# A four-fold row fold for the Fourier step of sketched attention, with mirrored output rows and a new order of issue

## The chip, the cores and the metric

The kernel runs on one NeuronCore of one Trainium2 chip. The metric is the device time of one execution in microseconds (us). The engines are TensorE (PE, with its weight loads PEld), VectorE (DVE), ScalarE (ACT), GpSimd (POOL) and SyncE (SP, which issues most DMAs).

## What is computed

Linear attention with sketched features, for batch 4, 4 heads, 1088 rows and head width 32, then a Fourier mix and a small MLP on rows of 128 (cut from the reference):

```
phi(x) = outer(S1 x, S2 x)                     # 8 x 8 = 64 features
kv = sum_s phi(k) v ;  z = sum_s phi(k)
attn = (phi(q) kv) / (phi(q) z + 1e-6)         # heads side by side: x is (4, 1088, 128)
mixed = real(fft(fft(x, axis=1), axis=2))
u = x + mixed
un = (u - mean(u)) / sqrt(var(u) + 1e-6)
out = u + relu(un @ w_ch1) @ w_ch2             # 128 -> 512 -> 128
```

## The kernel before

All work is a list of named steps (`add(name, engine, reads, writes, emit)`). `ORDER` is a list of all step names written out by hand: the instructions of each engine, and the DMAs of SP's queue, are issued in that order. `ENGINE` moves a step to another engine than its default, `BANK` gives each PSUM use its bank, `BEHIND` makes a load wait for an earlier DMA of SP's queue, `AFTER` adds single waits, and `FILL` puts matmuls on zeros (`zeros`, L88 and L90) in front of a step.

**Attention.** For each batch b, `ld_k`, `ld_v` and `ld_q` (L123, L127, L141) load the inputs, DVE transposes k and q in blocks of 32 (`kT`, L379; `qT`, L428), PE makes the features (`kproj`, L361; `qfeat`, L435), ACT copies them out of PSUM (`kab`, `qa`), and POOL or DVE forms the products (`kp`, L102; `qp`, L446). PE sums kv and z (`kv`, L395), and numerator and denominator (`pnd`, L481). DVE takes the reciprocal (`rden`, L493) and writes x in bf16 (`xx`, L496). Each half of the 1088 rows gives four tiles, rows 4p to 4p + 3 on partition p; the 32 rows left of each half (`ld_qt`, `qt_T`, `qt_f`, `qt_a`, `qt_p`) form a ninth tile.

**Row transform.** `dfold` (df) adds and subtracts mirrored columns of x (nine tiles, 567 columns an instruction), and `fold` (eo) adds and subtracts the halves, rows r and r + 544 (516 columns), which leaves four tiles for even and four for odd frequencies. `srow` (s) multiplies them with tables of cosines and sines: for each of the four tiles, and once for the ninth, six matmuls of 272 to 274 columns (L521), 30 for a batch. The tables come from `t_turn`, `t_ph`, `t_pm`, `t_sin`, `t_cos` and `t_neg`, those of the ninth tile from `l_...`. `zev` (z) copies the spectrum out of PSUM; `zrev` (zr) writes it once more backwards with signs for the second half of the rows; `zlast` (zl) picks the columns of the ninth tile.

**Mixer.** Groups g = 0 to 9 follow: for each batch and half a group of four tiles (g = 0, 1, 2, 3, 5, 6, 7, 8), and for each pair of batches a group of one tile (g = 4 and 9). In each, `mix` adds x and the column transform in PSUM (L574, L577), `bn`, `var`, `sd`, `rc` and `un` normalize, `xt` transposes by DMA on SP's queue (L635; g up to 6, later groups use PE: `tr` and `ut`), `ph` and `rl` are the hidden layer and its relu (L643, L650, L652), `po` adds the output layer into the same PSUM bank (L657), and `fin` copies it to an `ot` buffer, of which the large groups share four. `own` (L559) names the buffers in turn. Then SP stores: `st_main` (L668) one DMA of 256 KB, 128 partitions of 2 KB, for a large group; `st_half` (L664) two DMAs, one from SP and one from ACT, for g = 8; `st_last` (L672) four DMAs of 16 KB for a group of one tile. Their patterns in DRAM, outermost dimension first:

```
L668  [[4 * DM, 128], [1, 4 * DM]]
L665  [[4 * DM, 128], [1, 2 * DM]]
L672  [[HALF * DM, 2], [2 * DM, 16], [1, DM]]      # x 4
```

The stores stand in `ORDER`, and so on SP's queue, among the transposes: xt0, xt1, xt2, out0, xt3, xt4, xt5, xt6, out2, out3, out1, out4, out5, out6, out9, out7, out8.0, with out8.1 on ACT.

Of the kernel before, what the change touches and what calls it, by code (L numbers as in the profile page):

```python
# [17 lines left out]
DM = H * D  # L18
# [4 lines left out]
LAST = HALF - 512  # L23
QD = DM // 2
NK = HALF // 2 + 1
NB = NK // 2 + 1
BY_DMA = (0, 1, 2, 3, 4, 5, 6)
SPLIT = {}
TURNS = {"un": 5, "unT": 5, "ht": 3, "ot": 4, "st": 5, "sm": 5}
NXD = 1  # L30
# [14 lines left out]
def view(t, offset, dims, p0=0, n=128):  # L45

    a = t[:]
    step = a.ap[0][0]
    return bass.AP(tensor=a.tensor, offset=a.offset + p0 * step + offset,
                   ap=[[step, n]] + [list(d) for d in dims])  # L50
# [6 lines left out]
def program(nc, T, x, bank):  # L57
# [82 lines left out]
    def ld_q(b, half):  # L140
        return [nc.sync.dma_start(view(T(f"q_in{b % 3}"), 4 * H * D * half, [[4 * D, H], [1, 4 * D]], p, n),  # L141
                                  dram(x["q"], (b * H * S + half * HALF + 4 * p) * D, [[4 * D, n], [S * D, H], [1, 4 * D]]))
                for p, n in parts(f"ld_q{b}.{half}", 128)]

    def ld_qt():

        return [nc.sync.dma_start(view(T("qt_in"), 0, [[D, B * H], [1, D]], 32 * par + 16 * half, 16),  # L147
                                  dram(x["q"], (512 + HALF * half + par) * D, [[2 * D, 16], [S * D, B * H], [1, D]]))
                for par in range(2) for half in range(2)]
# [31 lines left out]
    def c_iota():  # L181
        first = nc.gpsimd.iota(T("pi")[:], pattern=[[0, 1]], base=0, channel_multiplier=1)

        nc.gpsimd.iota(T("sr")[:], pattern=[[1, 6]], base=0, channel_multiplier=4,
                       allow_small_or_imprecise_dtypes=True)
        return first
    add("c_iota", POOL, "", "iota", c_iota)

    def c_kk():
# [7 lines left out]
    add("c_rows", DVE, "iota", "rows", lambda: nc.vector.tensor_scalar(  # L197
        out=T("sq")[:, 0:4], in0=T("sr")[:, 0:4], scalar1=1.0 / S, scalar2=None, op0=ALU.mult))

    def c_more():  # L200
        v = nc.vector
        pi, pa, sr = T("pi"), T("pa"), T("sr")
        for i, bits in enumerate((15, 16, 32, QD - 1)):
            v.tensor_scalar(out=pa[:, i:i + 1], in0=pi[:], scalar1=bits, scalar2=None, op0=ALU.bitwise_and)

        v.tensor_scalar(out=sr[:, 5:6], in0=pa[:, 0:1], scalar1=2.0, scalar2=512.0, op0=ALU.mult, op1=ALU.add)
        v.scalar_tensor_tensor(out=sr[:, 5:6], in0=pa[:, 1:2], scalar=HALF / 16.0, in1=sr[:, 5:6], op0=ALU.mult, op1=ALU.add)
        v.scalar_tensor_tensor(out=sr[:, 4:5], in0=pa[:, 2:3], scalar=1 / 32.0, in1=sr[:, 5:6], op0=ALU.mult, op1=ALU.add)
        v.tensor_copy(sr[:, 5:6], pa[:, 3:4])
# [23 lines left out]


    base = lambda: view(T("kk"), 0, [[NK, 2], [1, NB]])
    for i, t in enumerate((0, 2, 1, 3)):
        add(f"t_turn{t}", POOL, "rows kk", f"pha/{t}", lambda i=i, t=t: turn(T("ph")[:, i, :], t, base(), S))
        add(f"t_ph{t}", DVE, f"pha/{t} rows", f"phb/{t}", lambda i=i, t=t: rest(T("ph")[:, i, :], t, base()))
    W = 2 * NB
    add("t_pm0", DVE, "phb/0 phb/2", "pm", lambda: size(T("pm")[:], T("ph")[:, 0:2, :]))  # L240
    add("t_sin0", ACTE, "phb/0 phb/2 tabsin", "tab/S0", lambda: sin(view(T("tab"), W, [[4 * W, 2], [1, W]]), T("ph")[:, 0:2, :], S))
    add("t_cos0", ACTE, "pm hpi tabsin", "tab/C0", lambda: cos(view(T("tab"), 0, [[4 * W, 2], [1, W]]), T("pm")[:], S))
    add("t_sin1", ACTE, "phb/1 phb/3 tabsin", "tab/S1", lambda: sin(
        view(T("tab"), 3 * W, [[4 * W, 2], [1, W]]), view(T("ph"), 3 * W, [[-W, 2], [1, W]]), S))
    add("t_cos1", ACTE, "phb/1 phb/2 phb/3 tabsin", "tab/C1", lambda: sin(
        view(T("tab"), 2 * W, [[4 * W, 2], [NB, 2], [1, NB]]), view(T("ph"), 2 * W + NB - 2, [[W, 2], [NB + 1, 2], [-1, NB]]), S))


    add("a_sin", ACTE, "hpi", "tabsin", lambda: nc.scalar.activation(out=T("scr")[:, 0:1], in_=T("hpi")[:, 0:1], func=ACT.Sin))
    add("a_sqrt", ACTE, "hpi wd0 tab/S0 tab/S1 tab/C0 tab/C1 tabL/S tabL/C", "tabsqrt", lambda: nc.scalar.activation(  # L250
        out=T("scr")[:, 1:2], in_=T("hpi")[:, 0:1], func=ACT.Sqrt))

    def t_neg(engine):
        return (nc.vector if engine == DVE else nc.gpsimd).tensor_scalar(
            out=T("tab")[:, 8:12, :], in0=T("tab")[:, 4:8, :], scalar1=-1.0, scalar2=None, op0=ALU.mult)
    add("t_neg", eng("t_neg", DVE), "tab/S0 tab/S1 tab/C0 tab/C1", "neg", lambda: t_neg(eng("t_neg", DVE)))


# [12 lines left out]
    def d_trig():  # L271
        for c in range(2):
            lo, hi = slice(QD * c, QD * c + QD), slice(QD - QD * c, 2 * QD - QD * c)
            nc.scalar.activation(out=T("wd")[lo, c, :], in_=T("dpm")[lo, :], func=ACT.Sin, scale=-2 * PI / DM, bias=T("hpi")[lo, 0:1])
            nc.scalar.activation(out=T("wd")[hi, c, :], in_=T("dph")[hi, :], func=ACT.Sin, scale=-2 * PI / DM)
    add("d_trig", ACTE, "dphb dpm hpi tabsin", "wd0", d_trig)

    def d_alt(engine):

        done = []  # L280
        for c in range(2):
            p = QD - QD * c
            for i in range(2):
                done.append(memset(engine, view(T("wd"), DM * c + i, [[2, QD]], p, 1), 1.0 - 2 * i))
# [3 lines left out]
    add("d_alt", eng("d_alt", POOL), "wd0 sgn0", "wd", lambda: d_alt(eng("d_alt", POOL)))  # L288
    add("c_sgn", eng("c_sgn", POOL), "", "sgn0", lambda: memset(eng("c_sgn", POOL), T("sgn")[:], 1.0))
    def c_xd(i, e):  # L290
        memset(e, view(T(f"xd{i}"), 9 * (2 * QD + 1), [[1, QD - 1]]), 0.0)
        return memset(e, view(T(f"xd{i}"), QD, [[2 * QD + 1, 9]]), 0.0)
# [3 lines left out]
    for i in range(3):  # L296
        e = eng(f"c_eo{i}", POOL)
        add(f"c_eo{i}", e, "" if i < 2 else "tab/S0 tab/S1 tab/C0 tab/C1", f"eo0/{i}", lambda i=i, e=e: memset(e, view(T(f"eo{i}"), 2 * QD + 1, [[3 * QD, 8], [1, QD - 1]]), 0.0))
# [7 lines left out]
    add("c_id16", ACTE, "idb", "id16", lambda: nc.scalar.copy(T("id16")[:], T("idb")[0:16, 0:16]))  # L306

    def c_cen(engine):
        if engine == ACTE:
            nc.scalar.activation(out=T("cen")[:], in_=T("idb")[:], func=ACT.Identity, bias=T("less")[:, 0:1])  # L310
        else:
            nc.vector.tensor_scalar(out=T("cen")[:], in0=T("idb")[:], scalar1=-1.0 / DM, scalar2=None, op0=ALU.add)
    add("c_cen", eng("c_cen", ACTE), "idb hpi", "cen", lambda: c_cen(eng("c_cen", ACTE)))

    def c_mask():
# [6 lines left out]
    add("c_idb", POOL, "", "idb", lambda: eye(T("idb")[:], 128))  # L322

    add("c_qtp", eng("c_qtp", POOL), "", "qtp0", lambda: memset(
        eng("c_qtp", POOL), view(T("qtp"), 64, [[256, 4], [1, 128]]), 0.0))
# [8 lines left out]
    for i in range(2):  # L334
# [4 lines left out]
    add("s_t", PE, "s12/0 s12/1 id16 warm", "pST", lambda: nc.tensor.transpose(  # L339
        ps("st", 0, [[1, 16]]), T("s12")[:], T("id16")[:]), "st")  # L340
# [89 lines left out]
    def qfeat(b, pr):  # L430

        for w, src in enumerate(("sa", "sb")):
            for g in range(4):
                for h in range(2):
                    nc.tensor.matmul(  # L435
                        ps(f"q{b}.{pr}", 512 * g + 256 * w, [[1, 256]], 64 * h, 64),
                        view(T(src), 0, [[1, F]], 32 * g, 32),
                        view(T(f"qT{b % 2}"), 128 * (2 * pr + h), [[512, 2], [1, 128]], 32 * g, 32),
# [26 lines left out]
    def qt_p():  # L465

        for j in range(2):
            nc.vector.tensor_tensor(
                out=view(T("qtp"), 32 * j, [[256, 4], [192, 2], [1, 32]]), in0=ps("qt", 512 * j + 256, [[64, 4], [32, 2], [1, 32]]),
                in1=view(T("qta"), 256 * j, [[64, 4], [32, 2], [1, 32]]), op=ALU.mult)  # L470
    add("qt_p", DVE, "pqt qta qtp0", "qtp", qt_p, "qt:2")

    def pnd(b):
        for s in range(9):
            for pr in range(2):
                for c in range(2):
                    if s < 8:
                        w = view(T(f"qp{b % 2}"), 1024 * pr + 128 * s + 64 * c, [[1, 64]])
# [21 lines left out]

    def dfold(b, engine, w):

        X, Y = T(f"x{b}"), T(f"xd{b % NXD}")
        n = 2 * QD + 1
        if w == 0:
            copy(engine, view(Y, 0, [[n, 9], [2 * QD, 2]]), view(X, 0, [[DM, 9], [QD, 2]]))
        return tt(engine, view(Y, QD * w + 1, [[n, 9], [1, QD - 1]]), view(X, 1, [[DM, 9], [1, QD - 1]]),
                  view(X, DM - 1, [[DM, 9], [-1, QD - 1]]), (ALU.add, ALU.subtract)[w])

    def fold(b, engine, w):  # L510
        X, n = T(f"xd{b % NXD}"), 2 * QD + 1
        return tt(engine, view(T(f"eo{b % 3}"), 12 * QD * w, [[3 * QD, 4], [1, n]]), view(X, 0, [[n, 4], [1, n]]), view(X, 4 * n, [[n, 4], [1, n]]), (ALU.add, ALU.subtract)[w])

    def srow(b):


        def six(weights, movs, start, stop):
            for c, part in ((0, 0), (0, 1), (1, 1), (1, 0), (1, 2), (0, 2)):
                p, mov = QD * (c ^ (part > 0)), movs[c][part == 1]
                n = mov.ap[-1][1] * (mov.ap[-2][1] if len(mov.ap) > 2 else 1)  # L520
                nc.tensor.matmul(ps(f"z{b}", 512 * c + c, [[1, n]], p, QD), weights[c][:, QD * part:QD * part + QD], mov,  # L521
                                 start=start and part < 2, stop=stop, tile_position=(0, p), skip_group_check=True)

        six([view(T(f"xd{b % NXD}"), 8 * (2 * QD + 1), [[1, 3 * QD]])] * 2,
            [[view(T("tabl"), 2 * NK * trig + (NK - 1 if c == 0 else 0), [[1, NK + 1 - c]]) for trig in range(2)] for c in range(2)],
            True, False)

# [374 lines left out]
```

## Time and profile before

| what | us |
|---|---|
| median of three runs (82.05 to 82.67) | 82.61 |
| the profiled execution | 82.32 |
| its span, first to last instruction | 80.4 |
| PE busy | 69.6 |
| DVE busy | 65.0 |
| ACT busy | 49.5 |
| POOL busy | 45.2 |
| first output (out0) issued | 55.84 |
| last output (out8.1) issued | 77.57 |

A row of the timeline gives start, length, engine, line, operation and tiles. A digit of a DMA line is the busy share of the 16 DMA engines in one of 40 equal slices, in tenths (9 is 90% or more), and the GB/s line under it what they moved.

### The profile page before, as it was taken

Reading aid. Unit: us, or ns where it says so; the run is one execution under the profiler, and the core shown is the slowest. Engines: PE = TensorE matmul, PEld = TensorE weight load, DVE = VectorE, ACT = ScalarE, POOL = GpSimd, SP = SyncE. Lnnn points to the kernel's source line nnn. Section 1 sums busy time; section 2 is a strip of 40 time slices with the busy share of each in tenths; the row PEclk is TensorE's granted clock in tenths of the full one; section 3 lists DMA queues with packets and bytes.
Section 4 is the critical chain, followed back from the end, with each engine's and each line's share of the span. In section 5 each row is a group of like instructions: output and inputs, shape, how many; then the busy total and the mean of one; then the engine's idle time right before and its main releaser. Section 6 shows DMA issues by size and latency. Waiting matters only on the chain.

```text
span 80.4 us, 3294 instructions
## 1 busy us (share of the span) xinstructions
PE 69.6 (87%) x1368; PEld 52.0 (65%) x1375; DVE 65.0 (81%) x178; ACT 49.5 (62%) x85; POOL 45.2 (56%) x84
## 2 busy tenths in 40 slices
PE   4998693799999999999999999989997969797930
PEld 2323552489799766878788789956674837583720
DVE  5895879999869999999759699999878659894800
ACT  6244576475693645479692285609978548979530
POOL 6888579975857499597999619149850010000000
PEclk9999999999999999999999999999999999999999
DMA  0969998379929659556015003030500466133042
GB/s 8 270 174 269 229 288 208 53 208 229 227 44 310 207 144 292 151 125 212 0 34 43 0 8 65 8 65 0 177 19 16 95 190 253 29 130 138 24 176 90
DMA packets 16095, 10.47 MB, mean 130 GB/s; under 512 B 6864, under 2 KB 14544, under 8 KB 16080
## 3 DMA queue, kind: packets, MB, share of 16 engines
q1 hardware_dynamic: 15896, 10.13, 47.0%
q8 instruction: 10, 0.16, 0.8%
q10 hardware_dynamic: 184, 0.14, 0.5%
q14 instruction: 5, 0.04, 0.2%
HBM read 7.22 MB, written 2.23 MB: 117 GB/s over the span
## 4 chain that ended last, share of the span: by engine, by line
PE 48%; DVE 18%; DMA 11%; SPq 8%; ACT 7%; issue 4%; DVEq 0%; ACTq 0%
PE ps L481 9%; PE ps L395 8%; PE ps L435 7%; PE ps L657 6%; DMA t_qt_in<-in_q_dram 6%; PE ps L643 5%; DMA t_unT__166<-t_un__161 5%; PE ps L361 4%; SPq L141 3%; ACT t_ht__168 L650 3%; PE ps L521 2%; PE ps L458 2%; SPq L147 2%; DVE t_x__130 L496 2%; DVE t_x__131 L496 2%
## 5 line engine op out<-in xcount | busy, mean ns | idle before, releaser
L102 POOL TENSOR_TENSOR t_kp__119<-t_ab__117 128x512 f32<-128x512 f32 x7 | 7.3, 1068 | 1.5 <-ACT t_ab__117 L413 1.1
L650 ACT ACTIVATE t_ht__167<-ps 128x1024 bf16<-128x1024 f32 x6 | 6.0, 1022 | 1.6 <-PE ps L481 1.6
L102 POOL TENSOR_TENSOR t_kp__118<-t_ab__116 128x512 f32<-128x512 f32 x6 | 6.3, 1069 | 1.0 <-ACT t_ab__116 L413 1.0
L442 ACT COPY t_qa__122<-ps 128x1024 f32<-128x1024 f32 x4 | 4.1, 1013 | 3.1 <-DVE t_qp__124 L446 1.9
L650 ACT ACTIVATE t_ht__168<-ps 128x1024 bf16<-128x1024 f32 x4 | 4.1, 1024 | 2.9 <-PE ps L577 1.9
L442 ACT COPY t_qa__123<-ps 128x1024 f32<-128x1024 f32 x4 | 4.1, 1014 | 2.3 <-PE ps L435 2.3
L643 PEld LDWEIGHTS <-t_w1b 128*128 128x128 bf16 x40 | 3.0, 97 | 3.7 <-issue 1.5
L90 PE MATMUL ps<-t_wz 128*128 128x512 bf16 x12 | 5.0, 526 | 0.0
L481 PEld LDWEIGHTS ps<-t_kvz,t_qp__124 128*64 128x64 f32 x128 | 4.0, 137 | 0.9 <-ACT t_kvz L95 0.4
L481 PE MATMUL ps<-t_kvz,t_qp__124 128*64 128x66 f32 x128 | 4.4, 223 | 0.1
L395 PE MATMUL ps<-t_v__121,t_kp__119 128*64 128x33 f32 x128 | 4.3, 223 | 0.1
L102 POOL TENSOR_TENSOR t_eo__133<-t_xd__132 128x516 bf16<-128x516 bf16 x4 | 4.2, 1052 | 0.4 <-DVE t_xd__132 L102 0.3
L395 PEld LDWEIGHTS ps<-t_v__121,t_kp__119 128*64 128x64 f32 x128 | 4.1, 138 | 0.4 <-POOL t_zl__143 L96 0.4
L395 PE MATMUL ps<-t_v__120,t_kp__118 128*64 128x33 f32 x128 | 4.3, 223 | 0.0
L481 PEld LDWEIGHTS ps<-t_kvz,t_qp__125 128*64 128x64 f32 x128 | 3.9, 137 | 0.5 <-issue 0.4
L481 PE MATMUL ps<-t_kvz,t_qp__125 128*64 128x66 f32 x128 | 4.2, 223 | 0.0
L395 PEld LDWEIGHTS ps<-t_v__120,t_kp__118 128*64 128x64 f32 x128 | 4.1, 138 | 0.1
L650 ACT ACTIVATE t_ht__169<-ps 128x1024 bf16<-128x1024 f32 x4 | 4.0, 1027 | 0.0
L652 DVE TENSOR_SCALAR t_ht__168<-ps 128x1024 bf16<-128x1024 f32 x2 | 2.5, 1225 | 1.7 <-PE ps L657 1.0
L435 PE MATMUL ps<-t_qT__115,t_sa 32*64 32x256 f32 x64 | 2.8, 400 | 1.2 <-DVE t_qp__124 L446 1.2
L379 DVE STREAM_TRANSPOSE t_kT__112<-t_k_in__105 128x512 f32<-128x512 f32 (+1 forms) x3 | 2.7, 886 | 1.1 <-DMA t_k_in__105<-in_k_dram 1.1
L361 PE MATMUL ps<-t_sblk,t_kT__112 128*64 128x64 f32 x64 | 2.5, 226 | 1.1 <-DVE t_kT__112 L379 1.1
(266 smaller groups left out, 216.6 us busy)
## 6 DMA issues: line engine op xcount, KB each, us to landing
t_q_in__109<-in_q_dram SPq DMA_DIRECT2D x4, 256.0 KB, 3.3
t_v_in__107<-in_v_dram SPq DMA_DIRECT2D x8, 128.0 KB, 3.6
t_k_in__106<-in_k_dram SPq DMA_DIRECT2D x2, 512.0 KB
t_v_in__108<-in_v_dram SPq DMA_DIRECT2D x8, 128.0 KB, 3.3
t_k_in__105<-in_k_dram SPq DMA_DIRECT2D x2, 256.0 KB
t_q_in__110<-in_q_dram SPq DMA_DIRECT2D x2, 256.0 KB, 6.6
t_q_in__111<-in_q_dram SPq DMA_DIRECT2D x2, 256.0 KB
t_k_in__105<-in_k_dram SPq DMA_DIRECT2D x1, 512.0 KB
```

Source lines behind the costliest of these rows:

```text
L90: nc.tensor.matmul(T("ps")[:, free, :], w[:, 0:128], bass.AP(tensor=w.tensor, offset=w.offset, ap=[list(w.ap[0]), [0, 4], [1, 128]]), star ...
L102: return (nc.vector if engine == DVE else nc.gpsimd).tensor_tensor(out=out, in0=in0, in1=in1, op=op)
L361: nc.tensor.matmul(ps(use, 64 * t, [[1, 64]], 64 * c, 64), view(src, 128 * t + 64 * c, [[1, 64]]), T("sblk")[:], start=True, stop=True, ti ...
L379: nc.vector.transpose(view(T(f"kT{b % 2}"), 128 * lo, [[1, 128 * n]]), view(T(f"k_in{b % 2}"), D * lo, [[D, n], [8 * D, 4], [1, D]]))
L395: nc.tensor.matmul(ps(f"kv{b}", 33 * pr, [[1, 33]], 64 * c, 64), kp, v, start=(t == 0), stop=(t == 8), tile_position=(0, 64 * c), skip_gro ...
L435: nc.tensor.matmul(ps(f"q{b}.{pr}", 512 * g + 256 * w, [[1, 256]], 64 * h, 64), view(T(src), 0, [[1, F]], 32 * g, 32), view(T(f"qT{b % 2}" ...
L442: nc.scalar.copy(T(f"qa{pr}")[:], ps(f"q{b}.{pr}", 0, [[512, 4], [1, 256]]))
L481: nc.tensor.matmul(ps(f"nd{b}", 512 * (s // 3) + 132 * (s % 3) + 66 * pr, [[1, 66]], 64 * c, 64), w, view(T("kvz"), 132 * b + 66 * pr, [[1 ...
L496: nc.vector.tensor_tensor(out=view(T(f"x{b}"), 0, [[384, 3], [32, 12], [1, 32]]), in0=ps(f"nd{b}", 0, [[512, 3], [33, 12], [1, 32]]), in1= ...
L643: nc.tensor.matmul(ps(use, 128 * n * i, [[1, 128 * n]]), T("w1b")[:, 128 * c:128 * c + 128], own("unT", g)[:, 0:128 * n], start=True, stop ...
L650: nc.scalar.activation(out=out, in_=in_, func=ACT.Relu)
L657: nc.tensor.matmul(ps(u, ut_at(g, t), [[1, 128]]), view(own("ht", g), (128 if g % 5 == 4 else 512) * c + 128 * t, [[1, 128]]), T("w2b")[:, ...
```

## The change

Rows r, 544 - r, 544 + r and 1088 - r now lie on one partition, or on mirrored columns of it. Partitions 0 to 63 hold rows 1 + 4p on of a half, partitions 64 to 127 the rows from 288 of that half, whose order `qfeat` reverses with steps of -1. Rows 0 and 544, and 257 to 272 with their mirrors, are the ninth tile. A new fold, `mfold` (mf), adds and subtracts neighbouring tiles of x, mirrored rows; `dfold` and `fold` then run on fewer columns, and `srow` needs two sets of six matmuls and the ninth tile's six: 18 for a batch. The tables shrink, `t_far` mirrors them. `zev` writes the spectrum in two steps, in the order in which `mix` reads it; `zrev` is one copy, read backwards, and the signs are in a second set of column weights (`d_neg`). `zlast` reads PSUM. Each `ld_q` is two DMAs of 64 partitions, `ld_qt` is five, each `st` is two DMAs of 128 KB, and `st_last` is three. `ENGINE`, `FILL`, `BEHIND`, `AFTER`, `ORDER` and `BANK` are new throughout; `BY_DMA` is as before. The core of the diff:

```diff
     def ld_q(b, half):
-        return [nc.sync.dma_start(view(T(f"q_in{b % 3}"), 4 * H * D * half, [[4 * D, H], [1, 4 * D]], p, n),
-                                  dram(x["q"], (b * H * S + half * HALF + 4 * p) * D, [[4 * D, n], [S * D, H], [1, 4 * D]]))
-                for p, n in parts(f"ld_q{b}.{half}", 128)]
+        return [nc.sync.dma_start(view(T(f"q_in{b % 3}"), 4 * H * D * half, [[4 * D, H], [1, 4 * D]], 64 * far, 64),
+                                  dram(x["q"], (b * H * S + half * HALF + (FAR if far else 1)) * D,
+                                       [[4 * D, 64], [S * D, H], [1, 4 * D]])) for far in range(2)]
...
+    def mfold(b, engine, w):
+        X = T(f"x{b}")
+        return tt(engine, view(T(f"xm{b % NXM}"), 5 * DM * w, [[DM, 5], [1, DM]]), view(X, 0, [[2 * DM, 5], [1, DM]]),
+                  view(X, DM, [[2 * DM, 5], [1, DM]]), (ALU.add, ALU.subtract)[w])
...
-        use = (((0, 0), (1, 1)), ((2, 11), (7, 2)), ((4, 8), (5, 9)), ((10, 3), (3, 6)))
-        for t in range(4):
-            six([view(T(f"eo{b % 3}"), 3 * QD * (4 * c + t), [[1, 3 * QD]]) for c in range(2)],
...
+        table = ((2, 0), (1, 3))
+        for a in range(2):
+            six(lambda c, part: view(T(f"eo{b % 3}"), 6 * QD * c + 3 * QD * a + QD * part, [[1, QD]]),
+                [[view(T("tab"), W * table[a][trig] + TW * (1 - c), [[1, NK - c]]) for trig in range(2)] for c in range(2)],
+                False, a == 1)
...
+    def zev(b, half, engine):
+        copy(engine, view(T(f"z{b}"), 256 * half, [[128, 2], [64, 2], [1, 64]]),
+             ps(f"z{b}", *((512, [[-511, 2], [1, 2], [2, 64]]) if half == 0 else (783, [[-512, 2], [-1, 2], [-2, 64]]))))
     def zrev(b, engine):
+        return copy(engine, view(T(f"z{b}"), 512, [[128, 4], [1, 128]]), view(T(f"z{b}"), 127, [[128, 4], [-1, 128]]))
...
-    def st_main(b, half, g):
-        return [nc.sync.dma_start(dram(x["out"], (b * S + half * HALF) * DM, [[4 * DM, 128], [1, 4 * DM]]),
-                                  own("ot", g)[:])]
+    def st(b, half, g, w):
+        row = ((1, HALF + 1), (HALF + FAR, FAR))[half][w]
+        return (nc.sync, nc.scalar)[g == TWO and w == 1].dma_start(
+            dram(x["out"], (b * S + row) * DM, [[2 * DM, 2], [4 * DM, 64], [1, 2 * DM]]), own("ot", g)[:, 256 * w:256 * w + 256])
     def st_last(i, g):
-        return [nc.sync.dma_start(dram(x["out"], ((2 * i + j // 2) * S + 512 + j % 2) * DM, [[HALF * DM, 2], [2 * DM, 16], [1, DM]]),
-                                  own("ot", g)[32 * j:32 * j + 32, 0:128]) for j in range(4)]
+        def rows(first, n, p0):
+            return nc.sync.dma_start(dram(x["out"], (2 * i * S + first) * DM, [[2 * DM, n], [HALF * DM, 4], [1, DM]]),
+                                     own("ot", g)[p0:p0 + 4 * n, 0:128])
+        return [rows(257, 16, 64), rows(258, 15, 4), rows(0, 1, 0)]
...
 FILL = {
-    "warm": (1, 1, 6), "qf0.1": (0, 2, 6), "qf0.0": (0, 3, 6), "kpr1": (0, 1, 7), "po8.0": (0, 1, 0),
+    "s_t": (1, 0, 0), "qf0.1": (1, 1, 0), "qf1.0": (0, 2, 6), "kt_pr": (0, 1, 6), "pnd0": (0, 2, 5), "pnd1": (0, 2,
+    4), "po8.0": (0, 1, 2),
 }
```

The new order of the first loads on SP is k0.1, S1, q0.0, q0.1, q1.0, q1.1, k0.0, k1, v0.1, qt, kt. On PE the first output layer, po0, stands behind s1 and ahead of mix4, mix2, pnd3, ph1, mix3, s2 and ph4.0; po1, mix5, po4 and ph2.0 follow that. The stores and transposes on SP now come as xt0, xt1, out0, xt4, xt2, xt3, out4, xt5, out1, xt6, out2, out5, out3, out6, out9, out7, out8.0, with out8.1 on ACT.

## The prediction

> **What bounds the kernel now.** I read the page first, then the table of stages, the chain in order of time, the SP queue in the timeline, and the DMA view of two short windows. The profiled execution took 82.32 us, 0.29 under the median of 82.61; its span is 80.4, so 1.92 lies around it. I sum against 82.32.
>
> ```profile
> span 80.4 us, 3294 instructions
> ...
> PE 69.6 (87%) x1368; PEld 52.0 (65%) x1375; DVE 65.0 (81%) x178; ACT 49.5 (62%) x85; POOL 45.2 (56%) x84
> ...
> PE 48%; DVE 18%; DMA 11%; SPq 8%; ACT 7%; issue 4%; DVEq 0%; ACTq 0%
> ```
>
> ```profile
> 20.00:30.00 10.00, 9.94 (x293) 8.25 (x289) 8.78 (x12) 6.16 (x12) 6.84 (x17) 1.00 0.66 186
> 30.00:40.00 10.00, 10.00 (x268) 7.90 (x267) 9.46 (x22) 7.04 (x11) 8.31 (x10) 1.00 0.54 160
> 40.00:50.00 10.00, 9.59 (x239) 8.29 (x232) 8.38 (x22) 5.70 (x9) 7.54 (x11) 1.00 0.20 28
> 50.00:60.00 10.00, 9.29 (x143) 7.50 (x142) 8.89 (x38) 6.59 (x14) 6.39 (x9) 1.00 0.22 57
> 60.00:70.00 10.00, 8.48 (x99) 6.01 (x98) 7.76 (x30) 7.44 (x13) 0.42 (x2) 1.00 0.39 116
> 70.00:80.40 10.40, 6.30 (x72) 4.47 (x72) 5.02 (x17) 5.56 (x9) 0.00 (x0) 1.00 0.31 109
> ```
>
> The columns after the length are PE, PEld, DVE, ACT, POOL, the granted clock, the DMA share and GB/s. From 20 to 40 us PE is never free, so there each PE instruction saved is time saved; from 60 on no engine is full and latencies decide. The clock is 1.00 throughout. In the last 30 us the DMA engines are used at a third: outputs are free today. The chain has the transform once:
>
> ```profile
> 32.52 1.76 PE ps L521 x30
> ```
>
> The DMA rows matter most. First the end of three whole outputs (L668) and the four small DMAs of L672, then the last two outputs (L664):
>
> ```profile
> 66.40 2.69 SPq L672 DMA_DIRECT2D out_dram<-t_otl__182  x4
> ```
>
> ```profile
> DMA  9989998997510111111100001111111000011111
> GB/s 410 410 307 410 478 375 307 410 444 273 171 35 0 34 34 34 34 43 51 34 9 0 0 0 43 26 43 34 51 34 43 0 0 0 17 34 26 43 43 43
> ```
>
> ```profile
> DMA  0000069999999989999999510000000000000000
> GB/s 0 0 0 0 0 241 386 386 410 361 361 386 410 338 253 349 361 362 326 337 337 361 181 24 0 0 0 0 0 0 0 0 0 0 0 0 0 0 0 0
> ```
>
> The first window is 67.0 to 69.4 us, 0.06 us a digit; the second 77.0 to 80.4, 0.085 a digit. A whole output, whose DRAM pattern begins with 128 rows, moves at 300 to 440 GB/s with all 16 engines busy (digit 9). An L672 DMA, whose DRAM pattern begins with a dimension of 2, moves at about 40 GB/s with one tenth of the engines busy: 40 against 360 is 1.8 of 16, so two engines. The first of them also starts only when the outputs before it are through (67.7, issued from 66.4): later DMAs queue behind earlier ones. [...]
>
> **The change, part by part.**
>
> Transform (srow, L521): 30 matmuls a batch become 18. 1.76 us / 30 = 58.7 ns; 12 x 4 x 58.7 ns = 2.82 us of PE. s0 and s1 lie in the full stretch: -1.41. s2 and s3 lie where PE has gaps: between -1.41 and 0; I take -0.7.
>
> Fillers (zeros): pnd0 and pnd1 get two matmuls each where kpr1 had one; one costs 0.32 on the chain (16.82): +1.0. A float32 filler stands before s_t and one before qf0.1; its nearest row, the two float32 matmuls of L351, takes 1.06. PE is idle 2.2 us of the first 10, so 0 to +2.1; I take +0.5.
>
> Folds: mf is new, 640 columns; df falls from 567 to 315 columns and eo from 516 to 258. POOL takes 1.27 for 567 columns, so mf 1.43, df 0.71, eo 0.53. Before, x0 to s0 cost POOL 1.26 + 0.23 + 1.26 + 2.06 = 4.8; after, with mf0.0 on DVE (0.46 to 0.55 for 567), 1.43 + 0.23 + 1.42 + 1.06 = 4.1. For batches 0 and 1, PE's own queue covers it; for 2 and 3, -0.7 to +0.7. I take 0.
>
> Tables: two turns leave POOL (2 x 0.93), two rests and t_neg leave DVE (1.0 + 0.89), two sines leave ACT (1.4). t_far comes to POOL (0.85 to 2.1, from L217 and L545) and ACT (1.2, from L543), with c_idb and c_jdb on ACT (0.39 each, L310), c_x9 and d_neg on POOL (some 1.4). Covered by the PE-full stretch: 0.
>
> Spectrum: zev becomes two reads of 256 (0.37 each by L95) for one of 0.75 to 0.79; zrev one copy of 512 (0.6 to 1.05) for 0.7 to 2.05; zlast four small DVE reads (0.2 each) for 0.4 to 1.4. Taken as 0, between -0.5 and +0.5. qt_p has four DVE instructions for two (+0.2, covered by kv0). qfeat, mix and pnd keep their instructions; only patterns change, and steps of -1 in a matmul have no row here: 0 to +0.5, taken 0. Two more relus on DVE (2 x 1.23, freeing 2 x 1.02 of ACT) fall where DVE is half idle: 0, or 0.5 either way.
>
> Loads: each ld_q is two DMAs (8 more issues at 0.45) and ld_qt five for four (0.6): 4.2 us more of SP's queue, which has no gap in the first 8 us. ld_q0.1 stood first and was in SBUF by 3.76; now k0.1, S1 and ld_q0.0 (four issues) stand before it, some 2 us. qf0.1, at 6.50 now, starts 0 to 2 later; I take +0.8. ld_qt ends some 1.6 later, but qt_f now stands behind kpr1, which covers it.
>
> Order: pnd3 (2.26), s2 (1.76), mix2 and mix3 (1.1) and a part of ph1 (0.3) were ahead of po0 on PE and now follow it. fin0 ended at 55.81; it ends at 55.8 - 5.4 + (-1.41 + 1.0 + 0.5 + 0.8) = about 51.3, and out0 is issued at about 51.
>
> Everything but the outputs: 82.32 - 1.41 - 0.7 + 1.0 + 0.5 + 0.8 = 82.5, plus or minus 2.
>
> Outputs: each of the eight whole outputs becomes two DMAs of 128 KB with a DRAM pattern that begins with 2. One engine moves 360 / 16 = 22 GB/s, so 64 KB on each of two engines take 2.95 us and an output 5.9, against some 0.7 now. If all use the same two engines, that is 8 x 5.9 = 47.2 us in one line, starting at 51. If each takes another pair, they run side by side, and only the last pays (2.95 for some 0.7). No row shows two of these DMAs in flight at once; I take the same pair, as nothing in the rows shows that a queue changes its engines. The new st_last begins with 16, 15 and 4 and gets quick; it is small.
>
> Who waits: the transposes (xt, L635) are on SP's queue behind the outputs. out0 is through at 51 + 0.8 (issue to first byte, 76.60 to 77.43) + 5.9 = 57.7; xt4, issued next, lands at 58.7 instead of 55.6. PE would reach ph4.0 at about 56 (after pnd3, ph1, mix3, s2) and sits there; mix5 follows at 60.3, bn5 to un5 3.6 more (bn5 to un5 now: 56.91 to 60.47), xt5 1.2: out1 is issued at about 65. From then on seven outputs (out1, 2, 5, 3, 6, 7, 8) keep the two engines busy: each fin finds its ot buffer (four of them) in time, since compute, held by xt6 behind out1, is still ahead of the line. 65 + 0.8 + 7 x 5.9 + 1.5 (xt5, xt6) = 108.6; the last byte stands 1.45 before the end of the span now (78.95 to 80.4): 110.1; with 1.92 outside, 112. Without any idle of the two engines after out0: 51 + 0.8 + 47.2 + 3.9 (four transposes of 0.9, as from 57.7 to 58.6 now, and the small xt4) + 1.45 + 1.92 = 106.3. I take 110, nearer the waiting end because the stall at ph4.0 has its own row of reasons.
>
> **Rivals.** (1) Successive output DMAs take different pairs of engines, or the pattern is spread over 16 after all: then nothing queues, and the time is 82.5 less what the new order regains of the 6.3 us that PE idles after 50, plus up to 2.2 for the last output: about 81, from 78.5 to 84. It ends on the other side: it decides from the point where a group's bytes drain faster than groups are made, under some 3 us a group (now seven are issued in 13.1 us, 64.49 to 77.57). For it: no row shows two such DMAs at once. Against it: L672's four DMAs, a tenth of the engines each. (2) The two DMAs of a group run side by side on two pairs: 2.95 a group, the stall shorter by as much, out1 at 62: 62 + 0.8 + 20.7 + 1.5 + 1.45 + 1.92 = 88. For it only that they are issued 0.4 us apart. (3) The outputs are spread and the start decides: 4.2 us of issue in front of the first loads, all of it lost with the fillers' 2.1: 82.5 + 3.4 + 0.8 = 86 to 87; against it PE's 2.2 us of early idle.
>
> **How the numbers follow.** Forecast 0.82; rival 1 0.11, of it 0.06 faster, 0.03 within 1%, 0.02 slower; rival 2 0.05; rival 3 0.02. About 1% is what a measurement of this kernel can tell from no change. So faster 0.06, same 0.03, slower 0.91. Predicted 110. Low: out0 at 49, no idle, engines at 24 GB/s (43.7 for 47.2): 106.3 - 2 - 3.5 = 101. High: out1 at 67, engines at the 20 GB/s of the L672 rows (6.5 an output): 67 + 0.8 + 45.5 + 1.5 + 1.45 + 1.92 = 118. The range 101 to 118 leaves out the rivals (0.18).
>
> **What would show it.** Right: after about 50 us the DMA line shows digits 1 and about 45 GB/s for some 50 us without a break, 9 gone; the transposes after out0 and out1 land 5 us or more after issue; PE, ACT and DVE are done some 15 us before the span's end, with fin8 waiting for out3; L521 has 72 matmuls instead of 120. Wrong: output bursts at 90 GB/s (two pairs) or 300 and more (spread), or the last output's landing within 3 us of its issue. If out1 comes near 58, the stall was too dear; if the 45 GB/s is 60, the engines were.

## The result, and the profile after

The changed kernel takes 116.78 us (median of 4 runs, 114.55 to 118.31) where the kernel before takes 82.33 (4 runs, 81.27 to 82.67): a ratio of 1.4075 with an interval of 1.3721 to 1.4428. The prediction said 110 and 101 to 118. The profiled execution took 115.33 us with a span of 113.5. Part of the runs, of the kernel before too, show a lower granted clock: the ratios leave those runs out, a kernel with too few others has its fastest run given instead of a ratio, and four profiles (stores undone, stores done, early q, q on ACT's queue) come from such a run.

The page of the changed kernel: the span, the engines, the granted clock, the DMA busy share and the GB/s, 2.8 us a slice.

```profile
span 113.5 us, 3252 instructions
...
PE 75.4 (66%) x1326; PEld 53.8 (47%) x1326; DVE 64.8 (57%) x197; ACT 47.8 (42%) x88; POOL 48.6 (43%) x92
...
PEclk9999769999999999999996569996569996555555
DMA  3679955655778304130165102191111111311110
GB/s 69 176 204 320 157 130 136 168 161 136 275 184 270 100 9 100 44 49 10 49 83 27 36 23 50 33 86 41 54 36 41 48 48 48 66 51 48 48 48 27
```

PE fell from 87% of the span to 66%, and no other engine took its place. After the last 9, at 74 to 77 us, the DMA line is 1 but for one 3 and the closing 0, and the GB/s are mostly 48: the kernel waits for transfers that use a small part of the DMA engines, a share of 0.14 at 48 GB/s from 100 to 112 us. The view of the DMA engines from 70 to 112 us, 1.05 us a digit, shows how long:

```profile
DMA  6111891111111111111111111143211111111111
```

The 6 at its start and the 8 and 9 fall on transposes, the 4, 3 and 2 on the stores of the small ninth tile; all else is 1.

SP's queue of the changed kernel (start, duration of the issue, what). L710 is the store `st`, two DMAs an output; L679 is the transpose `xt`.

```profile
52.02 1.21 SPq L710 DMA_DIRECT2D out_dram<-t_ot__167  x2
53.69 1.14 SPq L679 DMA_TRANSPOSE t_unTl__177<-t_unl__175  x1
...
70.03 1.61 SPq L710 DMA_DIRECT2D out_dram<-t_ot__168  x2
71.77 2.20 SPq L679 DMA_TRANSPOSE t_unT__159<-t_un__154  x1
74.07 2.75 SPq L710 DMA_DIRECT2D out_dram<-t_ot__169  x2
...
88.41 5.25 SPq L710 DMA_DIRECT2D out_dram<-t_ot__168  x2
...
100.29 4.04 SPq L710 DMA_DIRECT2D out_dram<-t_ot__170  x1
```

out0 is issued at 52.0 (51 was forecast) and out1 at 70.0 (65 was forecast). Behind each stands a transpose, and the chain of waits of the changed kernel passes through both, and then through out3, whose buffer the last group has to write:

```profile
53.69 7.89 DMA t_unTl__177<-t_unl__175
...
71.77 6.80 DMA t_unT__159<-t_un__154
...
84.60 11.56 DMA out_dram<-t_ot__170
...
96.23 0.37 ACT t_ot__170 L96
```

The second number is the time from issue to landing. The last computing instruction ends at 96.6, and 17 us later the span does. The stages (length, PE, PEld, DVE, ACT, POOL, granted clock, DMA share, GB/s):

```profile
60.00:70.00 10.00, 8.37 (x74) 6.09 (x74) 4.21 (x19) 4.25 (x8) 3.40 (x11) 0.66 0.14 22
70.00:80.00 10.00, 4.99 (x36) 2.62 (x36) 5.16 (x18) 4.17 (x9) 1.21 (x6) 0.87 0.48 63
80.00:90.00 10.00, 8.97 (x84) 6.91 (x83) 6.09 (x18) 6.17 (x10) 0.00 (x0) 0.78 0.13 43
...
100.00:112.00 12.00, 0.00 (x0) 0.00 (x0) 0.00 (x0) 0.00 (x0) 0.00 (x0) 0.50 0.14 48
```

PE looks busy from 60 to 70, but with 74 matmuls at a granted clock of 0.66: behind its waits for the two transposes it runs slower for a while here, at 0.54 from 60 to 65 us and at 0.50 from 78.6 to 82.2. `po` (16 matmuls, L701), 1.00 us at 50.38 in the chain, took 1.71 at 62.23. One of the experiments has the same first wait without the lower clock.

### The profile page after: what moved, and what is told of

Its sections match the earlier page's. It is cut to its first block, busy times and chain, and to the rows that moved or that the text cites. A ratio compares the mean times of both kernels' runs of the same rounds, so it can differ in the third digit from the quotient of the medians.

```text
span 113.5 us, 3252 instructions
## 1 busy us (share of the span) xinstructions
PE 75.4 (66%) x1326; PEld 53.8 (47%) x1326; DVE 64.8 (57%) x197; ACT 47.8 (42%) x88; POOL 48.6 (43%) x92
## 4 chain that ended last, share of the span: by engine, by line
PE 30%; DMA 29%; DVE 14%; SPq 6%; issue 4%; ACT 2%; DVEq 0%; ACTq 0%
DMA out_dram<-t_ot__170 10%; DMA t_unTl__177<-t_unl__175 7%; DMA t_q_in__110<-in_q_dram 6%; DMA t_unT__159<-t_un__154 6%; PE ps L687 4%; PE ps L701 4%; PE ps L425 4%; SPq L143 4%; PE ps L465 4%; PE ps L519 3%; PE ps L565 3%; PE ps L391 2%; DVE t_qp__125 L477 2%; DVE t_qT__116 L458 2%; PE ps L616 2%
## 5 line engine op out<-in xcount | busy, mean ns | idle before, releaser
L687 PEld LDWEIGHTS <-t_w1b 128*128 128x128 bf16 x40 | 3.5, 109 | 13.5 <-DMA t_unT__159<-t_un__154 4.5
L103 POOL TENSOR_TENSOR t_kp__120<-t_ab__118 128x512 f32<-128x512 f32 x7 | 7.3, 1064 | 3.8 <-DVE t_pm L236 2.8
L103 POOL TENSOR_TENSOR t_kp__119<-t_ab__117 128x512 f32<-128x512 f32 x7 | 7.3, 1067 | 1.5 <-ACT t_ab__117 L443 1.5
L103 POOL TENSOR_TENSOR t_xd__134<-t_xm__133 128x315 bf16<-128x315 bf16 x7 | 5.5, 785 | 2.5 <-PE ps L565 2.1
L687 PE MATMUL ps<-t_unT__159,t_w1b 128*128 128x512 bf16 x8 | 3.1, 505 | 4.4 <-DMA t_unT__159<-t_un__154 4.4
L694 ACT ACTIVATE t_ht__164<-ps 128x1024 bf16<-128x1024 f32 x5 | 5.1, 1028 | 1.3 <-PE ps L675 1.0
L694 ACT ACTIVATE t_ht__166<-ps 128x1024 bf16<-128x1024 f32 x3 | 3.1, 1024 | 6.0 <-PE ps L687 6.0
L694 ACT ACTIVATE t_ht__165<-ps 128x1024 bf16<-128x1024 f32 x4 | 4.1, 1031 | 2.3 <-PE ps L687 2.3
L701 PE MATMUL ps<-t_w2b,t_ht__165 128*128 128x128 bf16 x48 | 4.9, 282 | 0.0
L701 PEld LDWEIGHTS <-t_ht__165 128*128 128x128 bf16 x48 | 4.4, 132 | 0.9 <-issue 0.6
L696 DVE TENSOR_SCALAR t_ht__166<-ps 128x1024 bf16<-128x1024 f32 x1 | 1.2, 1224 | 5.3 <-PE ps L687 5.3
```

The source lines that it names most:

```text
L103: return (nc.vector if engine == DVE else nc.gpsimd).tensor_tensor(out=out, in0=in0, in1=in1, op=op)
L687: nc.tensor.matmul(ps(use, 128 * n * i, [[1, 128 * n]]), T("w1b")[:, 128 * c:128 * c + 128], own("unT", g)[:, 0:128 * n], start=True, stop ...
L694: nc.scalar.activation(out=out, in_=in_, func=ACT.Relu)
L701: nc.tensor.matmul(ps(u, ut_at(g, t), [[1, 128]]), view(own("ht", g), (128 if g % 5 == 4 else 512) * c + 128 * t, [[1, 128]]), T("w2b")[:, ...
```

## The experiments

The theory: the DRAM pattern of `st` begins with 2, so each DMA runs on two engines, always the same two, and 256 KB take over 5 us; the outputs form one line, and what is issued behind them on SP's queue waits. The rivals: something else in the change (the new order, the doubled loads, the fillers) makes the slowdown, or the two engines are not the same for each DMA.

**The DMA by itself.** A kernel that stores the output from a constant tile and computes nothing, in four phases that wait for each other: a leading 2 from SP; a leading 2 from SP and ACT in turn; a leading 4; a leading 16.

```
LEAD = (2, 2, 4, 16)
e = nc.scalar if b == 1 and w % 2 else nc.sync
e.dma_start(dram(out, (b * S + 256 * w) * DM, [[2 * DM, c], [2 * c * DM, 128 // c], [1, 2 * DM]]), ot[:, 256 * w:256 * w + 256])
```

> Stores alone, nothing computed, all outputs written with ones: four phases, each of four DMAs of 128 KB and one small one, each phase after the one before has landed. The outermost DRAM dimension is 2 in phase 1 (all issued by SP), 2 in phase 2 (issued by SP and ACT in turn), 4 in phase 3 and 16 in phase 4, with 64, 64, 32 and 8 rows inside. Theory (as many engines as the outermost dimension, and always the same ones): 48, 48, 97 and 360 GB/s, so 10.8, 10.8, 5.4 and 1.4 us of transfer. If DMAs in flight use different pairs: up to 190 GB/s in phase 1 or 2. If the two queues have different pairs: 97 GB/s in phase 2 alone.

The page of that kernel, 1.08 us a slice; the phases begin at 2, 15.5, 29.5 and 37.6 us:

```profile
DMA  0001111111411100113111111110122342007740
GB/s 0 0 2 29 31 49 47 48 48 47 74 49 49 40 0 14 31 35 51 53 47 49 47 48 48 47 43 0 21 82 95 94 105 96 24 4 195 199 119 0
```

Leading 2: 48 GB/s. Leading 2 from two queues: 48 again, where DMAs on two different pairs would give 96. Leading 4: 95. Leading 16: 195 and 199, where 360 was expected; SP took 2.52 us to issue these four DMAs (4 x 128 KB in 2.52 us are 208 GB/s), so this phase does not show what sixteen engines move. So twice the leading dimension moves twice the bytes, 24 GB/s for each unit of it at 2 and at 4, and with a leading 2 a second queue adds nothing: the line shows 1 and 48 GB/s in both phases, so the two queues share their engines. That a unit is one engine is an estimate from the busy shares: 0.14 of 16 engines, 2.2 of them, at 48 GB/s in the changed kernel from 100 to 112 us, and 0.28, 4.5 of them, in the third phase from 30 to 37 us, its small DMA included. Which engines they are, no run here shows.

**The stores alone undone.** The changed kernel with the same bytes stored by 64 partitions, the pattern's leading dimension 64, still two DMAs an output.

```diff
-            dram(x["out"], (b * S + row) * DM, [[2 * DM, 2], [4 * DM, 64], [1, 2 * DM]]), own("ot", g)[:, 256 * w:256 * w + 256])
+            dram(x["out"], (b * S + rows[0] + 2 * i) * DM, [[4 * DM, 64], [(rows[1] - rows[0]) * DM, 2], [1, 2 * DM]]),
+            own("ot", g)[64 * i:64 * i + 64, :]) for i in range(2)]
```

> The changed kernel with only the pattern of the large stores changed: a group is stored by 64 partitions at a time with the 64 rows outermost in DRAM (two DMAs of 128 KB a group as before, four of 64 KB for g = 8), so that the outermost dimension is 64 and not 2. If the two-engine line is the whole loss (my theory), the time is the forecast's sum without outputs, 82.5 plus or minus 2, the DMA line shows bursts of 300 GB/s or more, and xt4 lands within 3 us. If the number of DMAs and their 1 KB packets cost the time (rival), it stays above 100. If the folds, the tables or the new order cost it (rival), it stays above 90 with PE, DVE or POOL as full as in the changed kernel up to 50 us.

The fastest of 4 runs took 86.76 us (to 90.86), beside 82.39 for the kernel before (7 runs, to 89.04). PE, which waited 3.3 us for the transpose behind out0 in the changed kernel, has no wait for it here, and the one behind out1 lands 2.47 us after its issue instead of 6.80:

```profile
70.89 2.47 DMA t_unT__159<-t_un__154
```

So the pattern is the bulk of the loss, but some 4 us stay, and 86.76 is above the "82.5, plus or minus 2" of the prediction. From 70 to 80 us the DMA engines have a share of 0.53 and move 123 GB/s. The 300 that were expected in bursts are more than SP issues in a row: it takes 0.6 to 0.65 us for 128 KB, which is 200 to 220 GB/s. The first place to look for the 4 us is SP's queue and the stages of this kernel:

```profile
1.73 2.73 SPq L143 DMA_DIRECT2D t_q_in__110<-in_q_dram  x4
4.51 2.59 SPq L143 DMA_DIRECT2D t_q_in__111<-in_q_dram  x4
```

```profile
25.00:30.00 5.00, 3.03 (x64) 2.31 (x66) 3.62 (x7) 2.63 (x3) 0.83 (x2) 0.77 0.73 211
30.00:35.00 5.00, 5.00 (x87) 4.10 (x86) 2.87 (x4) 1.90 (x4) 4.76 (x6) 0.55 0.63 188
```

Eight loads of q keep SP for 5.4 us at the start; at 25 us PE waits 2.3 us for q of batch 2, and then runs at a granted clock of 0.55. That low clock is of this execution and not of the kernel: the changed kernel, the same up to out0, has 0.76 from 10 to 15 us and 1.00 from 20 to 60 in its profile.

**The stores alone done.** The kernel before, with nothing but this pattern in its large stores, two DMAs an output (rows come out in another order within each half).

```diff
-        return [nc.sync.dma_start(dram(x["out"], (b * S + half * HALF) * DM, [[4 * DM, 128], [1, 4 * DM]]),
-                                  own("ot", g)[:])]
+        return [d for c in range(2) for d in st_half(b, half, g, c)]
...
-            dram(x["out"], (b * S + half * HALF + 2 * c) * DM, [[4 * DM, 128], [1, 2 * DM]]), own("ot", g)[:, 256 * c:256 * c + 256])]
+            dram(x["out"], (b * S + half * HALF + 256 * c) * DM, [[2 * DM, 2], [4 * DM, 64], [1, 2 * DM]]), own("ot", g)[:, 256 * c:256 * c + 256])]
```

> The kernel before with only its large stores changed: each as two DMAs of 128 KB whose DRAM pattern begins with a dimension of 2, as in the changed kernel; the rows of the output are permuted within each half by it. Theory: the output line alone makes it slow. xt3 to xt6 queue behind out0 alone (5.4 us at the 48.5 GB/s of the changed kernel), then seven outputs in one line from about 65: 65 + 0.8 + 7 x 5.4 + 2 + 1.5 + 1.9 = 109, range 103 to 113. Rival (the changed kernel is slow for its folds or its order): 82 to 86.

116.33 us (114.12 to 118.1), ratio 1.3771 (1.3371 to 1.4171): the old computation in the old order is nearly as slow as the changed kernel. The expected 103 to 113 was too low: the line of seven outputs begins at 71.2 us (out2) and not at 65, which is most of the difference. In front of it out0 is issued at 57.95, 2.1 us later than in the kernel before, and the transpose behind it lands only 7.27 us after its issue; later the chain has a wait for an output buffer:

```profile
59.26 7.27 DMA t_unT__165<-t_un__160
...
79.11 10.53 DMA out_dram<-t_ot__171
```

**Half of the outputs.** The two-engine pattern for groups 5 to 8 alone, then for groups 0 to 3 alone, all other stores by 64 partitions.

```diff
+        if g >= 5:
+            return [(nc.sync, nc.scalar)[g == TWO and w == 1].dma_start(
+                dram(x["out"], (b * S + rows[c]) * DM, [[2 * DM, 2], [4 * DM, 64], [1, 2 * DM]]),
+                own("ot", g)[:, 256 * c:256 * c + 256]) for c in ((w,) if g == TWO else range(2))]
```

The other kernel has `g < 5` in its place.

> As e1_sixteen, but the stores of g = 5, 6, 7 and 8 keep the pattern that begins with 2: half the dose, and no DMA transpose behind it but those already issued. Theory: the four outputs are one line of 4 x 5.4 = 21.6 us from the issue of out5, about 67: 67 + 0.8 + 21.6 + 1.5 + 1.9 = 93, range 88 to 97. Rival (loss is not in the stores): as e1_sixteen within 1 us. Rival (a queue changes its engines from DMA to DMA): within 3 us of e1_sixteen.

> The changed kernel with the large stores spread over sixteen engines for groups 5 to 8, and with the two-engine pattern kept for groups 0 to 3 alone. Theory (each two-engine output holds its two engines 5.4 us, and the transposes issued behind it on SP's queue cannot land before it): out0 delays the transpose behind it by 3 to 5 us, out1 and out2 the next one by 4 to 5 us, and out3 holds the buffer that the last group writes: 94 us (91 to 97) where the version with all stores spread takes 87 to 90. Rival (only the pile at the end counts, since the early stores have work beside them): within 1.5 us of the version with all stores spread. In the trace the DMA transposes behind out0 and out1 land over 5 us after issue if the theory holds, and 2.5 us after if the rival does.

Groups 5 to 8: 102.4 us (101.24 to 106.58), ratio 1.2174 (1.1967 to 1.2381). Groups 0 to 3: 97.28 us (96.64 to 102.79), ratio 1.1859 (1.1761 to 1.1957). Both are above what was expected, the second just past its range, the first by far. In that one the line begins at 71.66 us (out5) and not at 67, since the version with all stores spread takes about 87 and not 82.5; and from there to the end of the span it takes 28.2 us and not the 23.9 of the sum; where those 4.3 us go stays open. The early outputs are not covered: the chain of the kernel with groups 0 to 3 has both transposes as late as the changed kernel has them, which the rival excluded:

```profile
54.86 7.90 DMA t_unTl__177<-t_unl__175
...
70.47 6.79 DMA t_unT__159<-t_un__154
...
82.77 7.67 DMA out_dram<-t_ot__170
```

In the kernel with groups 0 to 3 the granted clock stays at its highest digit until 78 us (2.4 us a slice):

```profile
PEclk9999999999999999999999999999999995899985
```

PE waits 3.3 us for the transpose behind out0 here too, as in the changed kernel, but its clock does not fall behind that wait, and out1 is issued 6.0 us after that transpose has landed, where the changed kernel took 8.4. So the lower clock costs about 2.4 us there, and the wait alone does not bring it about; what does stays open.

And in the kernel with groups 5 to 8, out3, which is stored by 64 partitions but issued behind the two-engine out5, lands only after 9 us, and the last group waits for its buffer:

```profile
73.56 9.01 DMA out_dram<-t_ot__170
```

What holds it there is not shown.

**The rest of the loss: the loads of q.** Four kernels. First the version with all stores spread, and each half of q in one load of 128 partitions:

```diff
-                                       [[4 * D, 64], [S * D, H], [1, 4 * D]])) for far in range(2)]
+                                       [[4 * D, 128], [S * D, H], [1, 4 * D]]))] * 2
```

> The version with all stores spread over sixteen engines, and each half of q loaded by one DMA of 128 partitions instead of two of 64: it leaves the regrouping of the far rows out (the upper 64 partitions get rows 257 and up, so other rows are computed), and issues 8 DMAs of q where 16 were issued. Theory A (what is left of the slowdown, 4 to 7 us, lies in the loads: SP issues 16 loads of q at 0.6 us each, and PE waits 4.2 us for q behind them): 84 us (82.5 to 86), with PE's waits for the q transposes at 15 to 30 us gone and the granted clock at 1.0 there. Theory B (the new order of issue, not the number of loads, makes PE wait): within 1 us of the version with all stores spread, measured at 86.8 to 90.9.

83.39 us (82.35 to 84.83), ratio 1.0088 (1.0013 to 1.0163). PE's waits for the q transposes are 1.3 us, and the granted clock is 1.0 up to 70 us. At the start one load of 128 partitions is issued in 0.48 to 0.53 us, two of 64 take 1.3:

```profile
1.74 0.95 SPq L143 DMA_DIRECT2D t_q_in__110<-in_q_dram  x2
2.73 1.06 SPq L143 DMA_DIRECT2D t_q_in__111<-in_q_dram  x2
```

With 16 loads PE's wait for q differs from profile to profile: 4.2 us with all stores spread, 3.2 with groups 0 to 3, 1.1 in the changed kernel. The time at which out0 is issued is a steadier measure, as these kernels differ ahead of it in the loads of q alone:

| kernel | DMAs of q | out0 issued, us |
|---|---|---|
| the changed kernel | 16 | 52.02 |
| two-engine stores for groups 0 to 3 | 16 | 53.19 |
| two-engine stores for groups 5 to 8 | 16 | 51.27 |
| stores spread, one load for each half of q | 8 | 49.10 |
| one load and one store (last experiment) | 8 | 49.91 |

So the doubled loads cost 1.4 to 4.1 us by then.

Second, the kernel before with its q loads split so, and nothing else:

```diff
-SPLIT = {}
+SPLIT = {f"ld_q{b}.{half}": (64, 64) for b in range(4) for half in range(2)}
```

> The kernel before, with each of its eight loads of q issued as two DMAs of 64 partitions, in the same places; the loads that wait for an earlier one wait for the same one as before. Theory A (the number of loads is the cost): 84 to 86 us, SP's issue of q twice as long, PE waiting for the first q transposes by 1 to 2 us more and for later ones too. Theory B (order and not number): within 1% of the kernel before, 82 to 83.2 us.

85.06 us (84.14 to 89.03), ratio 1.0333 (1.0238 to 1.0428): the number of loads costs in the old order too, 2.7 us; out0 is issued at 58.27 instead of 55.84.

Third, the version with all stores spread, and the late load of q for batch 2 put ahead of three loads of v:

```diff
-ld_v1.0 qT1.0 qT1.1 qa0.1 l_cos ld_v1.2 ld_v1.3 qp0.1 ld_q2.1 ld_v1.1 qf0.0 qa0.0 kT0.0 kpr0.1 kpr0.0 kab0 l_sin
+ld_q2.1 ld_v1.0 qT1.0 qT1.1 qa0.1 l_cos ld_v1.2 ld_v1.3 qp0.1 ld_v1.1 qf0.0 qa0.0 kT0.0 kpr0.1 kpr0.0 kab0 l_sin
```

> The version with all stores spread over sixteen engines, and the second half of q for batch 2 issued ahead of three loads of v instead of behind them; nothing else moves. If the place of that load in SP's queue is what makes PE wait 2.3 us at 25 us and run at half the granted clock until 36 us, it goes: 85.5 us (84 to 87.5), the load issued at about 18.8 us instead of 21.2. If the wait is the number of loads and their traffic, the load only trades places with those of v: within 1 us of the version with all stores spread (86.8 to 90.9).

88.27 us (86.29 to 89.59), ratio 1.0599 (1.0437 to 1.0762). The fastest run is at 86.29, beside 86.76 for the version with all stores spread. PE's wait for q is 1.2 us instead of 4.2, but it waits 1.1 for k (`kT`) and 0.7 for x: the time stays, as if the loads only traded places. With its ratio this kernel also stands for the version with all stores spread, which had none.

Fourth, the second load of each pair issued from ACT's queue:

```diff
-        return [nc.sync.dma_start(view(T(f"q_in{b % 3}"), 4 * H * D * half, [[4 * D, H], [1, 4 * D]], 64 * far, 64),
+        return [(nc.sync, nc.scalar)[far].dma_start(view(T(f"q_in{b % 3}"), 4 * H * D * half, [[4 * D, H], [1, 4 * D]], 64 * far, 64),
```

> The version with all stores spread over sixteen engines, and the second of each pair of q loads (the far rows) issued from ACT's queue instead of SP's: the same 16 loads of 64 partitions, the same bytes. Theory A1 (the cost of the doubled loads is SP's time to issue them, 0.6 us each, which pushes the loads behind them back): SP issues the last load of q at 22 us instead of 24 to 27, PE's waits for q go, and the time falls from 88 us towards the 83.4 us measured with one load of 128 partitions for each half: 84.5 us (83 to 86). Theory A2 (a load of 64 partitions is slower to move, whoever issues it): stays at 86.5 to 89 us, with PE waiting for q as long as before.

The fastest of 6 runs took 87.65 us (to 90.21): no gain, against the theory that it is SP's issue time. But the kernel does not settle it. ACT issues the first of its loads of q only at 3.92 us, and SP waits from 5.65 to 12.23 for one of ACT's loads, by a wait that `BEHIND` sets:

```profile
3.92 1.47 ACTq L143 DMA_DIRECT2D t_q_in__110<-in_q_dram  x2
```

```profile
5.15 0.50 SPq L124 DMA_DIRECT2D t_k_in__107<-in_k_dram  x1
12.23 0.33 SPq L128 DMA_DIRECT2D t_v_in__108<-in_v_dram  x1
```

So it is shown that 16 loads for 8 cost some 3 to 4 us here, and it stays open how much of that is the issue and how much the transfer.

**What the arithmetic is worth.** One load for each half of q, and one store for each output (two for the last):

```diff
-            dram(x["out"], (b * S + rows[0] + 2 * i) * DM, [[4 * DM, 64], [(rows[1] - rows[0]) * DM, 2], [1, 2 * DM]]),
-            own("ot", g)[64 * i:64 * i + 64, :]) for i in range(2)]
+            dram(x["out"], (b * S + rows[0]) * DM, [[2 * DM, 128], [(rows[1] - rows[0]) * DM, 2], [1, 2 * DM]]),
+            own("ot", g)[:, :])]
```

> One load of 128 partitions for each half of q, and one store of 128 partitions for each output (two for the last group, as in the kernel before): it leaves the regrouping of far rows and the order of the rows in the output out, so that it computes and writes other rows, with the arithmetic, its order and the bytes as in the changed kernel. If the number of DMAs is all that the changed kernel pays for beyond the two-engine stores, what is left is the shorter row transform: the version with one load and two stores took 83.4 us beside 83.9 of the kernel before, its last group ended 0.9 us earlier than that of before and its last stores 1.3 us later, so 81.5 us (80.5 to 82.5), under the kernel before by 0.5 to 1.5 us. Rival (the new order of issue costs what the shorter transform saves): 82.5 to 84 us, no different from the kernel before.

81.48 us (80.82 to 83.72), ratio 0.9903 (0.9839 to 0.9966), so about 1% under the kernel before. It writes rows to other places, so it is a measure, not a version to use. Its last group's copy starts at 76.82, later than in the kernel with two stores (76.23), and yet the span ends at 80.1 instead of 80.8, as the last two stores are issued in 0.35 to 0.40 us each. In the version with two DMAs an output:

```profile
75.66 1.32 SPq L714 DMA_DIRECT2D out_dram<-t_ot__169  x2
77.08 1.20 SPq L711 DMA_DIRECT2D out_dram<-t_ot__170  x2
```

With one:

```profile
76.25 0.40 SPq L714 DMA_DIRECT2D out_dram<-t_ot__169  x1
76.82 0.35 SPq L711 DMA_DIRECT2D out_dram<-t_ot__170  x1
```

The steps from 0.9903 to 1.0088, 1.0599 and 1.4075, each times 82.33, give the account: new arithmetic, order and fillers -0.8 us; stores as two DMAs +1.5; loads of q as two DMAs +4.2; the leading 2 of the stores +28.6. The ratios come from several chips, with intervals of about 0.6 to 3.5% either way, so the smaller terms are good to a microsecond or so. The 4.2 of the loads stands beside the 1.4 to 4.1 by the time of out0 and the 2.7 in the old order.

## Why the prediction was right, and where its steps were off

The mechanism was the forecast one. Two engines, the same ones for each DMA, one line of outputs, transposes behind it, the last group waiting for out3, PE, ACT and DVE done 17 us before the end (some 15 forecast): each is in the runs, and undoing the pattern alone removes some 28 us. That successive DMAs use the same two engines was a choice for which the profile before had no row, though the 47.2 us of the sum rest on it; the stores by themselves showed it, with 48 GB/s for four DMAs of one queue and 48 for two queues. Which two engines these are, no run shows. Rivals 1 and 2, spread or different pairs, are excluded by the 48 GB/s of both phases with a leading 2. Rival 3, spread stores and a start that decides, was put at 86 to 87 us, and the version with all stores spread takes about that. This is in part luck: with 4.2 in place of 0.8 for the loads and 2.1 in place of 0.5 for the fillers its sum is 87.5, it had nothing for the number of stores (1.5), and whether the issue of the loads is the cost stays open. That the doubled loads cost some microseconds was right, and hidden behind the larger loss.

Terms of the sum that were off:

- **An output**: 5.9 us forecast, at 22 GB/s an engine. Measured 48.5 GB/s, 24 an engine by the shares above; 256 KB / 48.5 GB/s = 5.4 us. Seven outputs made 3.5 us too much.
- **The transpose behind out0**: forecast to land at 58.7, one microsecond after the output. It landed at 61.6. From the issue of out0 to this landing 9.6 us passed for 7.7 forecast, and out0 itself was 1.0 later. The transpose behind out1 took 6.80 us from issue to landing, and 2.47 behind a spread output: 4.3 more. Of the 9.6 us, the 0.8 to the first byte and the 5.4 of an output, by estimate, leave 3.4, where the prediction added 1.0 for the transpose, which is too little.
- **out1**: forecast at 65, issued at 70.0. 2.9 us of that were there when the transpose landed. From its landing to out1 8.4 us passed for 6.3 forecast; in that stretch PE ran at a granted clock of 0.54 to 0.77, which the prediction did not have. The kernel with groups 0 to 3, at full clock there, took 6.0.
- **The line after out1**: forecast to end at 110.1, 45 us after out1; the span ended at 113.5, 43.5 us after it. Here the faster engines gave back a part. About 2 us of their 3.5 were lost again, where the line ran low: 31 to 33 GB/s from 72 to 73.5 us, and 23 to 37 from 83.5 to 86, since out5 was issued only at 82.85. The prediction had compute ahead of the line throughout.
- **Everything but the outputs**, 82.5 plus or minus 2: too low. The version with all stores spread stands at a ratio of 1.06, about 87. The loads were put at +0.8, from the wait for the first q alone; they cost +4.2 by the ratios, 2.7 in the old order, and PE waits for later q as well. Up to out0 this hardly shows, 52.0 for a forecast of about 51, as the rest ahead of out0 was quicker than its forecast: with 8 loads out0 comes at 49.1 to 49.9. Stores as two DMAs, counted with the outputs only by their bytes, cost 1.5 at the end even when spread. The transform's -2.8 is there (18 matmuls in 1.17 to 1.25 us, 30 in 1.76 before), but with the fillers and the order only 0.8 us of it is left, against the -0.6 that the terms without the loads came to.

In total: the sum with the wait was 112; out1 5 us later and the line 1.5 us shorter make 115.5, and the profiled execution took 115.33. The 110 was that sum lowered by 2 towards the case without idle, which the transposes do not allow.

## What to carry to other kernels

Before a change that splits a tile's partitions into groups, write down the DRAM pattern of every load and store that it makes, and look at the first dimension: with 64 rows first and then 2 the kernel ended some 28 us sooner than with 2 first, for the same bytes. A slow store costs more than its own time where transposes or buffers stand behind it in the same queue; look at what the first ones delay (here two transposes, which landed after 7.89 and 6.80 us) as much as at the pile at the end, and do not count on a spread DMA to pass them: out3 took 9.01 us behind a two-engine out5. Then count the DMAs: here twice the loads and stores cost more (4.2 and 1.5 us by the ratios) than a transform that lost 40% of its matmuls gained (2.8).

## What the runs showed that was not expected

- An issue took longer while the line was long: a single store took SP 4.04 us to issue at 100.29, where the kernel with one spread store an output issues in 0.35 to 0.58. In the changed kernel the two stores at 88.41 took 5.25, and SP issued nothing else before 93.76: the slow line cost SP's time here, and not only that of the bytes.
- A load of 64 partitions took longer to issue (0.6 to 0.65 us in the first 8 us, the very first 0.76) than one of 128 partitions with twice the bytes (0.48 to 0.53 in the first 4).
- In some executions PE's granted clock was low behind a wait, which made it dearer than its length: 0.54 from 60 to 65 us in the changed kernel, behind 3.3 us (po 1.71 us for 1.00). In the kernel with groups 0 to 3 it stayed at 1.00 behind a wait of the same length.
